# A kernel whose order comes from a planner: new job lengths, new hand-offs and new ranks

## The chip, the core and the metric

One core of a Trainium2 chip runs the whole program. Its engines are named as in the profile: PE (TensorE, matrix products), PEld (PE's weight loads), DVE (VectorE), ACT (ScalarE), POOL (GpSimd) and SP (SyncE, which only issues transfers here). The metric is the device time of one launch in microseconds (us), as the median of several runs; lower is better. A profiled execution gives the trace that is read below.

## The reference, cut to what matters

```python
x = attention(q, k, v)              # (2, 12, 448, 64), causal, softmax over keys
x = x.transpose(0, 2, 1, 3).reshape(896, 768)
h = x @ w_in                        # 768 -> 2048
P = a[0] + a[1]*h + a[2]*h*h + a[3]*h**3
Q = 1.0 + abs(b[0])*abs(h) + abs(b[1])*h*h
x = (P / (Q + 1e-6)) @ w_out        # 2048 -> 768
gate = 1.0 / (1.0 + exp(-(x @ w_gate)))
out = (gate * (x @ w_val)) @ w_out2 # 768 -> 1536 -> 768
```

Attention comes first, then a feed-forward layer with a rational function (weights `in`, `out`), then a gated one (weights `gate`, `val`, `out2`).

## The kernel before

**Attention** works on twelve pairs of heads, numbered 0 to 11: six for the first batch of tokens, six for the second. The 448 tokens are cut into four row tiles of 112, gathered in three groups: row tiles 0 and 1, row tile 2, row tile 3. A pair goes through these steps. PE makes the scores of a group (`s`, line 442). DVE adds the mask and takes the maximum of each row (`e`, `sc`, line 450). ACT takes the exponential (line 464). PE transposes the result (`p`, line 482). DVE copies the first and third group out of PSUM (line 492), ACT the second (line 490). PE multiplies by v, one product for each of four key tiles (`x`, line 519, of 448, 336, 224 and 112 columns). On the side DVE inverts the row sums (lines 470 and 471), PE spreads them (`r`, line 501), ACT copies them out (line 511), and DVE multiplies `x` by them (`xn`, line 528). ACT and POOL split the result into a high and a low part (`xh`, line 535; `xl`, line 540). There is one PSUM buffer for `x`: the first `x` product of the next pair has to wait until DVE's line 528 has read the last one. `s` and `p` share two PSUM buffers.

**Feed-forward products** come as triples high x high, high x low, low x high: `h` in lines 256 to 258, `o` in lines 314 to 316, `z` in lines 379 to 381. The first `h` and `o` tiles need only the first batch of tokens, so their triples are put between attention's matmuls and keep PE busy there. A weight is split on the way in: SP loads it, ACT takes two passes (lines 157 and 161), DVE joins the words (`val`, line 164), ACT or POOL rounds (lines 172 and 174) and POOL subtracts (line 176). ACT and DVE also evaluate the rational function on each `h` tile (lines 271 to 287).

**The order** on every engine is made while the program is built. Each step is a `Job` with an engine, a length in microseconds (`cost`), jobs that it waits for, and a rank. `in_turn` plays the jobs through: the engine that can start first takes, among its ready jobs, the one of lowest rank; a job's result is available to another engine a `handoff` later. The order that comes out is fixed in the program (each instruction is tied behind the one before it on its engine). On the chip an engine keeps that order and waits for real results, so the lengths decide the order alone and not the time. The ranks are `rank + R_...`, a pair's place in time plus an offset for each kind of step (`R_MAX`, `R_EXP`, `R_COPY`, `R_X` and so on); weight steps have `R_W`, `W_AT` and `W_STEP`.

Of the kernel before, what the change touches and what calls it, by code (L numbers as in the profile page):

```python
# [35 lines left out]
def in_turn(named, handoff):  # L36

    free = {}
    waiting = {}
    jobs = list({id(j): j for j in named.values()}.values())  # L40
    for j in jobs:
        deps = [named[d] for d in j.deps if d in named]
        j.waits = len(deps)
        for d in deps:
            d.then.append(j)
    for j in jobs:
        free.setdefault(j.engine, 0.0)
        waiting.setdefault(j.engine, [])
        if not j.waits:
            waiting[j.engine].append(j)  # L50
    for _ in jobs:
        now, e = min((max(free[e], min(j.ready for j in w)), e) for e, w in waiting.items() if w)
        job = min((j for j in waiting[e] if j.ready <= now), key=lambda j: j.rank)
        waiting[e].remove(job)
        free[e] = now + job.cost
        for j in job.then:
            j.ready = max(j.ready, free[e] + (handoff[e] if j.engine != e else 0.0))
            j.waits -= 1
            if not j.waits:
                waiting[j.engine].append(j)  # L60
        yield job
# [8 lines left out]
def tile_causal_attention__moe_rational__moe_glu(  # L70
# [16 lines left out]
    B, NP, P, _, S = qk.shape  # L87
    CP, NQ, _, D = v.shape[2:]
# [8 lines left out]
    NT = B * S  # L97
# [21 lines left out]
    for i in range(N_WARM):  # L119
# [7 lines left out]
        out=mask[:, S - CP :],  # L127
# [92 lines left out]
    CUT = S // P * P  # L220
# [189 lines left out]
    GROUPS = [(0, 1), (2,), (3,)]  # L410
# [132 lines left out]
    J = {}  # L543

    def job(key, engine, cost, deps, rank, emit, *args):
        J[key] = Job(engine, cost, deps, rank, lambda: emit(*args))
# [4 lines left out]
    def freed_by(ring, back=2):  # L551
        k = len(freed[ring]) - back
        return freed[ring][k] if k >= 0 else []
# [1 line left out]

    NG = len(GROUPS)
    LA = 2
    R_TURN, R_R, R_X, R_W = -11.0, -16.0, 34.0, -3.5
    R_MAX, R_COPY, R_INV, R_XN = -14.5, -9.5, 7.0, 12.5
    R_EXP, R_ROUT = 6.25, -42.5  # L560
    W_AT, W_STEP = 9, 5
    R_SUM = 9.5
    EXP = (0.39, 0.48, 0.57, 0.67)
    MAX = (0.28, 0.39, 0.51, 0.62)
    COPY = (0.39, 0.62, 0.70, 1.09)
    both = range(2)
    for it in range(len(pairs) * NG + LA):
        n, k = divmod(it, NG)
        rank = it * NQ / NG
        if n < len(pairs):  # L570
            if k == 0:
                job(("load", n), "SP", 3.0, [("x", n - 3, NQ - 1)], (n - 2) * NQ, load, n)
            job(
                ("s", n, k),
                "PE",
                sum(0.187 * (t + 1) + 0.05 for t in GROUPS[k]) + 0.25,
                [("load", n), *freed_by("s")],
                rank - 37.5,
                scores,
                n,  # L580
                k,
            )
            for t in GROUPS[k]:
                for j in both:
                    job(("max", n, t, j), "DVE", MAX[t] + 0.08, [("s", n, k), ("p", n - 1, k)], rank + R_MAX, maximum, n, k, t, j)
                    job(("exp", n, t, j), "ACT", EXP[t] + 0.19, [("max", n, t, j), ("r", n - 3)], rank + R_EXP, exponentials, n, t, j)
            freed["s"].append([("max", n, t, j) for t in GROUPS[k] for j in both])
        if it < LA:
            continue
        n, k = divmod(it - LA, NG)  # L590
        rank = (it - LA) * NQ / NG
        job(
            ("p", n, k),
            "PE",
            sum(0.2 * (t + 1) for t in GROUPS[k]) + 0.1,
            [("exp", n, t, j) for t in GROUPS[k] for j in both] + freed_by("s"),
            rank + R_TURN,
            turn,
            n,
            k,  # L600
        )
        for t in GROUPS[k]:
            job(("copy", n, t), "ACT" if t == 2 else "DVE", COPY[t], [("p", n, k), ("x", n - 2, NQ - 1)], rank + R_COPY, copied, n, k, t)
        freed["s"].append([("copy", n, t) for t in GROUPS[k]])
        if k < NG - 1:
            continue
        job(("inv", n), "DVE", 0.4, [("exp", n, t, j) for t in range(NQ) for j in both], rank + R_INV, inverses, n)
        job(("r", n), "PE", 0.9, [("inv", n), ("r out", n - 1)], rank + R_R, factors, n)
        job(("r out", n), "ACT", 0.52, [("r", n), ("hi", n - 1), ("lo", n - 1)], rank + R_ROUT, factors_out, n)
        for kt in range(NQ):  # L610
            deps = [("copy", n, t) for t in range(kt, NQ)] + [("x", n, kt - 1) if kt else ("xn", n - 1)]
            job(("x", n, kt), "PE", 0.187 * (NQ - kt) + 0.15, deps, rank + R_X + kt / 2, values, n, kt)
        job(("xn", n), "DVE", 0.62, [("x", n, NQ - 1), ("r out", n)], rank + R_XN, result, n)
        job(("hi", n), "ACT", 0.57, [("xn", n)], rank + 1, result_hi, n)
        final = pairs[n][1] == NP - 1
        job(("lo", n), "DVE" if final else "POOL", 0.62 if final else 1.14, [("hi", n)], rank + 1, result_lo, n)


    def coefficients():
# [18 lines left out]

    job("late", "", 0.0, [k for k in J if k != "ab"], 0, late)

    UNIT2 = 0.525
    UNIT = {S: 0.615, CUT: 0.525, NT - CUT: 0.69}

    STAGES = [("SP", 4.0), ("ACT", 0.92), ("ACT", 0.9), ("DVE", 1.3), ("ACT", 0.84), ("POOL", 2.0)]
    portions = []

    def portion(key, w, free, rank):
        p = len(portions)
        portions.append(key)
        for m, (engine, cost) in enumerate(STAGES):  # L650
            if m == 4 and key[0] in BY_POOL:
# [80 lines left out]
        follow(key, stages, rank, [*free, *deps])  # L732
        n_tmp.append((key, len(stages) - 1))

    RATIONAL = [("ACT", 1.9), ("DVE", 2.0), ("ACT", 1.28), ("DVE", 2.05), ("ACT", 0.56), ("POOL", 1.3)]
    GLU = [("ACT", 0.62), ("DVE", 0.62), ("ACT", 0.56), ("POOL", 1.25)]

    def scaled(stages, c, b, more=0.0):
        f = width(c, b) / S
# [2 lines left out]
    def stage_in(c, b):  # L742

        groups = [(0, 1), (2,), (3,)] if (c, b) == (0, 0) else [(i,) for i in range(NF)]
        for group in groups:
            keys = [("in", c, b, i) for i in group]
            deps = [place(k, 1) for k in keys]
            for u in range(KC):
                for k, d in zip(keys, deps):
                    w = [("in", c, k[3] // 2, u // 3, 5), ("lo", b * NP + u)]  # L750
                    matmuls(k, u, d + w, UNIT[width(c, b)], in1_tile)
            for k in keys:
                followed(k, scaled(RATIONAL, c, b), ("out", c, b, 0, "mm", k[3]))
            yield

    def stage_out(c, b):
        stages = [("ACT", 0.53) if c == 0 else ("DVE", 0.62)]
        if c == NCH - 1:
            stages += [("ACT", 0.56), ("POOL", 1.25)]
        for e in range(KC):  # L760
            key = ("out", c, b, e)
            deps = place(key, 0)
            for i in range(NF):
                matmuls(key, i, deps + [("out", c, i, 0, 5), ("in", c, b, i, "after", 5)], UNIT[width(c, b)], out1_tile)
            follow(key, scaled(stages, c, b, 0.15 * (c > 0) * b), at["end"] + R_SUM)
            yield

    def stage_in2(c, b):
        for i in range(NF2):
            kg, kv = ("gate", c, b, i), ("val", c, b, i)  # L770
            for key, make in ((kg, gate_tile), (kv, val_tile)):
                deps = place(kv, 0 if key == kg else 1)
                for u in range(KC):
                    w = [(key[0], c, 0, u // 3, 5), ("out", NCH - 1, b, u, "after", 2)]
                    matmuls(key, u, deps + w, UNIT[width(1, b)], make)

            followed(kv, scaled(GLU, 1, b), ("out2", c, ready[b], 0, "mm", i), [("in", NCH - 1, 1, NF - 1, "after", 2)])
            yield

    def stage_out2(c, b):  # L780
        stages = [("ACT", 0.48) if c == 0 else ("DVE", 0.55)]
        if c == NCH2 - 1:
            stages.append(("SP", 0.1))

        sums = [("out", NCH - 1, k, KC - 1, "after", 2) for k in range(B)]
        for m in range(ready[b], ready[b + 1]):
            for n in range(2):
                key = ("out2", c, m, n)
                deps = place(key, 0) + sums
                for i in range(NF2):  # L790
                    gs = [("val", c, k, i, "after", 3) for k in range(b + 1)]
                    matmuls(key, i, deps + [("out2", c, i, 0, 5), *gs], UNIT2, out2_tile)
                follow(key, stages, at["end"] + R_SUM)
                yield
# [40 lines left out]
            j.rank = at[j.rank]  # L835

    latest = {}
    for j in in_turn(J, {"PE": 0.2, "DVE": 0.1, "ACT": 0.12, "POOL": 0.12, "SP": 0.1, "": 0.0}):
        traced = nc.cur_bb.bb.instructions
        before = len(traced)  # L840
        j.emit()
        for ins in traced[before:]:
            if ins.engine in latest:
                tc.add_manual_dep(
                    ins,
                    latest[ins.engine].name,
                    mybir.DependencyInfo(mybir.DependencyClass.NoSync, mybir.DependencyReason.DATA),
                    reason="in turn",
                )
            latest[ins.engine] = ins  # L850
# [43 lines left out]
```

## Time and profile before

| | us |
|---|---|
| median of 3 runs (602.89 to 604.39) | 602.94 |
| the profiled execution | 603.39 |
| its span, first to last instruction | 601.4 |
| PE busy | 593.5 (99%) |
| DVE busy | 358.0 (60%) |
| ACT busy | 357.2 (59%) |
| POOL busy | 254.4 (42%) |

The profiled execution took 603.39 us, of which 1.99 lie around the span. Attention's work ends about 126 us into the span; the rest is feed-forward work. A matmul's end is modelled in the profile, so PE's busy time also covers waits that are shorter than what the model adds; the chain of waits, which shows how far each piece carried the run forward, gives a better price for a block of matmuls.

### The profile page before, as it was taken

The numbers are of one execution on the slowest core, as the hardware profiler recorded it, in microseconds if no ns is written. First come the engines' busy times: TensorE is split into PE (matmuls) and PEld (weight loads), VectorE is DVE, ScalarE is ACT, GpSimd is POOL, SyncE is SP. The second block draws the span as 40 slices with busy tenths as digits, with TensorE's granted clock in tenths as the row PEclk, the third lists the DMA queues.
The fourth block names the chain that finished last, engine by engine and source line by source line (L and its number), as shares of the span: only waits on it lengthen the run. The fifth ranks groups of instructions, "written<-read, shape, count | busy, mean of one in ns | idle before, by whom it ended". The sixth has DMA issues, their size and how long they took to land.

```text
span 601.4 us, 8821 instructions
## 1 busy us (share of the span) xinstructions
PE 593.5 (99%) x3352; PEld 511.6 (85%) x3352; DVE 358.0 (60%) x677; ACT 357.2 (59%) x686; POOL 254.4 (42%) x193
## 2 busy tenths in 40 slices
PE   7999999999999999999999999999999999999997
PEld 5566666689988998898898989989989989989987
DVE  5877899938968986789685243246336335312314
ACT  6888888858897793859396448766344444111010
POOL 0634321357529656534746465545145144211010
PEclk9999999999999999999999999999999999999999
DMA  7645340045413351323421054645324123000004
GB/s 242 207 173 158 118 166 16 6 157 166 146 53 110 108 195 53 113 88 123 152 59 51 2 158 158 210 157 161 102 105 159 54 105 106 0 1 1 0 14 170
DMA packets 25641, 65.05 MB, mean 108 GB/s; under 512 B 1984, under 2 KB 3776, under 8 KB 25600
## 3 DMA queue, kind: packets, MB, share of 16 engines
q1 hardware_dynamic: 25600, 64.50, 32.7%
q8 instruction: 26, 0.43, 0.3%
q14 instruction: 15, 0.12, 0.1%
HBM read 61.74 MB, written 2.75 MB: 107 GB/s over the span
## 4 chain that ended last, share of the span: by engine, by line
PE 97%; DVE 2%; issue 0%; ACT 0%; DVEq 0%
PE h L256 7%; PE o L314 6%; PE h L258 6%; PE h L257 6%; PE o L315 6%; PE o L316 6%; PE z L381 5%; PE z L379 5%; PE z L380 5%; PE gu L257 5%; PE gu L258 5%; PE gu L256 5%; PE vu L257 5%; PE vu L256 5%; PE vu L258 5%; PE s L442 4%
## 5 line engine op out<-in xcount | busy, mean ns | idle before, releaser
L361 POOL TENSOR_TENSOR gl<-pr_u,gh 128x384 fp32r<-128x384 f32 (+1 forms) x24 | 27.7, 1153 | 111.5 <-ACT gh L359 111.5
L289 POOL TENSOR_TENSOR gl_h<-t_h,gh_h 128x384 fp32r<-128x384 f32 (+2 forms) x32 | 39.2, 1226 | 84.0 <-ACT gh_h L287 83.9
L256 PE MATMUL h<-xh,wh_in 128*128 128x384 f32 (+2 forms) x192 | 71.3, 371 | 0.0
L314 PE MATMUL o<-gh_h,oh_out 128*128 128x384 f32 (+2 forms) x192 | 70.3, 366 | 0.0
L315 PE MATMUL o<-gl_h,oh_out 128*128 128x384 f32 (+2 forms) x192 | 69.9, 364 | 0.0
L316 PE MATMUL o<-gh_h,ol_out 128*128 128x384 f32 (+2 forms) x192 | 69.9, 364 | 0.0
L258 PE MATMUL h<-xh,wl_in 128*128 128x384 f32 (+2 forms) x192 | 69.7, 363 | 0.0
L257 PE MATMUL h<-xl,wh_in 128*128 128x384 f32 (+2 forms) x192 | 69.7, 363 | 0.0
L176 POOL TENSOR_TENSOR ol_out<-val_out,oh_out 128x768 fp32r<-128x768 f32 x28 | 55.1, 1971 | 26.7 <-ACT oh_out L174 25.4
L389 DVE TENSOR_TENSOR y<-y,z 128x384 f32<-128x384 f32 x70 | 38.3, 552 | 32.2 <-PE z L381 32.1
L357 DVE TENSOR_TENSOR pr_u<-sg_u,vu 128x384 f32<-128x384 f32 (+1 forms) x24 | 14.8, 617 | 70.8 <-PE vu L258 68.4
L381 PE MATMUL z<-oh_out,gl 128*128 128x384 f32 x168 | 56.2, 335 | 0.0
L379 PE MATMUL z<-oh_out,gh 128*128 128x384 f32 x168 | 56.2, 335 | 0.0
L380 PE MATMUL z<-ol_out,gh 128*128 128x384 f32 x168 | 56.2, 334 | 0.0
L164 DVE SCALAR_TENSOR_TENSOR val_out<-raw_out 128x768 uint32<-128x768 uint32 x28 | 35.7, 1277 | 31.3 <-ACT raw_out L161 23.4
L464 ACT ACTIVATE e<-e,sc 112x112 f32<-112x112 f32 (+3 forms) x96 | 49.7, 522 | 6.5 <-DVE sc L450 6.3
L258 PE MATMUL gu<-xh,wl_gate 128*128 128x384 f32 (+1 forms) x144 | 52.2, 363 | 0.0
L257 PE MATMUL gu<-xl,wh_gate 128*128 128x384 f32 (+1 forms) x144 | 52.2, 363 | 0.0
L257 PE MATMUL vu<-xl,wh_val 128*128 128x384 f32 (+1 forms) x144 | 52.1, 362 | 0.0
L256 PE MATMUL gu<-xh,wh_gate 128*128 128x384 f32 (+1 forms) x144 | 52.1, 362 | 0.0
L256 PE MATMUL vu<-xh,wh_val 128*128 128x384 f32 (+1 forms) x144 | 52.1, 362 | 0.0
L258 PE MATMUL vu<-xh,wl_val 128*128 128x384 f32 (+1 forms) x144 | 52.1, 362 | 0.0
(89 smaller groups left out, 1425.5 us busy)
## 6 DMA issues: line engine op xcount, KB each, us to landing
raw_out<-in_moe_w_out_dram SPq DMA_DIRECT2D x28, 768.0 KB, 4.3
raw_in<-in_moe_w_in_dram SPq DMA_DIRECT2D x16, 768.0 KB, 4.5
raw_gate<-in_moe_w_gate_dram SPq DMA_DIRECT2D x12, 768.0 KB, 4.3
raw_val<-in_moe_w_val_dram SPq DMA_DIRECT2D x12, 768.0 KB, 4.3
qk<-in_qk_dram SPq DMA_DIRECT2D x12, 448.0 KB, 5.7
v<-in_v_dram SPq DMA_DIRECT2D x12, 224.0 KB, 3.8
out_dram<-y SPq DMA_DIRECT2D x14, 192.0 KB, 1.8
a_sb<-in_moe_a_dram SPq DMA_DIRECT2D x1, 2.0 KB, 7.1
```

What stands on the lines that cost most here:

```text
L176: nc.gpsimd.tensor_tensor(lo, vf, hi, op=ALU.subtract)
L256: nc.tensor.matmul(ps, hi[:, c, fs], xh[:, c, bs], start=(c == 0), stop=False)
L257: nc.tensor.matmul(ps, hi[:, c, fs], xl[:, c, bs], start=False, stop=False)
L258: nc.tensor.matmul(ps, lo[:, c, fs], xh[:, c, bs], start=False, stop=(c == KC - 1))
L289: nc.gpsimd.tensor_tensor(gl, t, gh, op=ALU.subtract)
L314: nc.tensor.matmul(ps, hi[:, es], gh, start=(i == 0), stop=False)
L315: nc.tensor.matmul(ps, hi[:, es], gl, start=False, stop=False)
L316: nc.tensor.matmul(ps, lo[:, es], gh, start=False, stop=(i == NF - 1))
L379: nc.tensor.matmul(ps, gh[:, ms], hi[:, ns], start=(i == 0), stop=False)
L380: nc.tensor.matmul(ps, gh[:, ms], lo[:, ns], start=False, stop=False)
L381: nc.tensor.matmul(ps, gl[:, ms], hi[:, ns], start=False, stop=(i == NF2 - 1))
L464: nc.scalar.activation(e, e, AF.Exp, bias=d["sc"][:, t, j : j + 1], scale=-1.0, accum_out=d["sum"][:, t, j : j + 1])
```

## The change

No instruction is added, removed or altered. The numbers in the planner are replaced: the lengths of jobs (an exponential loses the 0.19 that was added to it, a maximum its 0.08; DVE's joining of weight words goes from 1.3 to 0.95; ACT's weight passes from 0.92 and 0.9 to 0.83 and 0.81; the two long DVE jobs of the rational function from 2.0 and 2.05 to 1.82 and 1.85), the hand-offs (DVE 0.1 to 0.18, ACT 0.12 to 0.2, POOL 0.12 to 0.15, PE 0.2 to 0.15) and all rank offsets. Of the diff a few lines stand for the rest:

```diff
-    R_TURN, R_R, R_X, R_W = -11.0, -16.0, 34.0, -3.5
-    R_MAX, R_COPY, R_INV, R_XN = -14.5, -9.5, 7.0, 12.5
+    R_TURN, R_R, R_X, R_W = -11.5, -27.0, 32.5, -12.0
+    R_MAX, R_COPY, R_INV, R_XN = -25.5, -20.5, 26.0, 3.5
...
-                    job(("exp", n, t, j), "ACT", EXP[t] + 0.19, [("max", n, t, j), ("r", n - 3)], rank + R_EXP, exponentials, n, t, j)
+                    job(("exp", n, t, j), "ACT", EXP[t], [("max", n, t, j), ("r", n - 3)], rank + R_EXP, exponentials, n, t, j)
...
-    STAGES = [("SP", 4.0), ("ACT", 0.92), ("ACT", 0.9), ("DVE", 1.3), ("ACT", 0.84), ("POOL", 2.0)]
+    STAGES = [("SP", 4.0), ("ACT", 0.83), ("ACT", 0.81), ("DVE", 0.95), ("ACT", 0.75), ("POOL", 1.9)]
...
-    for j in in_turn(J, {"PE": 0.2, "DVE": 0.1, "ACT": 0.12, "POOL": 0.12, "SP": 0.1, "": 0.0}):
+    for j in in_turn(J, {"PE": 0.15, "DVE": 0.18, "ACT": 0.2, "POOL": 0.15, "SP": 0.1, "": 0.0}):
```

All five engines get a new order; three places of it follow. In the names the first number of `s_2_1`, `p_2_0`, `x_1`, `xn_...` and `e_2_3_0` counts pairs, the second of `s` and `p` is the group, the second of `e` the row tile; the last number only counts buffers.

The first place is PE from the third pair's last scores to the second pair's first `x` products. Before:

```order
L442 MATMUL s_2_2_374<-qk_0_2_181 112x448 x2
L482 MATMUL p_2_0_378<-ident_102,e_2_0_0_313 112x112
L482 MATMUL p_2_0_378<-ident_102,e_2_0_1_322 112x112
L482 MATMUL p_2_0_378<-ident_102,e_2_1_0_325 112x112 x2
L482 MATMUL p_2_0_378<-ident_102,e_2_1_1_337 112x112 x2
L519 MATMUL x_1_390<-pt_0_1_156,v_0_1_152 64x448 x2
L519 MATMUL x_1_390<-pt_0_1_156,v_0_1_152 64x336 x2
```

Now, on the same engine:

```order
L442 MATMUL s_2_2_360<-qk_0_2_184 112x448 x2
L482 MATMUL p_2_0_364<-ident_102,e_2_0_0_309 112x112
L482 MATMUL p_2_0_364<-ident_102,e_2_0_1_311 112x112
L482 MATMUL p_2_0_364<-ident_102,e_2_1_0_323 112x112 x2
L482 MATMUL p_2_0_364<-ident_102,e_2_1_1_325 112x112 x2
L519 MATMUL x_0_286<-pt_0_0_149,v_0_0_145 64x224 x2
L519 MATMUL x_0_286<-pt_0_0_149,v_0_0_145 64x112 x2
L482 MATMUL p_2_1_398<-ident_102,e_2_2_0_344 112x112 x3
L482 MATMUL p_2_1_398<-ident_102,e_2_2_1_350 112x112 x3
L519 MATMUL x_1_407<-pt_0_1_156,v_0_1_152 64x448 x2
```

The last two `x` products of pair 0, which stood far ahead of this place, have moved to just before the first of pair 1, with one transposition between them.

The second place is DVE at the same time, around line 528 of pair 0. Before:

```order
L164 SCALAR_TENSOR_TENSOR val_in0_0_3_372<-raw_in0_0_3_274 128x768
L528 TENSOR_TENSOR xn_0_266<-xn_0_266,x_0_288 128x448
L450 ISA e_2_3_0_388,sc_0_2_186<-s_2_2_374,mask_107 112x448
L450 ISA sc_0_2_186 112x1
L450 ISA e_2_3_1_395,sc_0_2_186<-s_2_2_374,mask_107 112x448
L450 ISA sc_0_2_186 112x1
L492 COPY pt_0_2_187<-p_2_0_378 112x2x112
L492 COPY pt_0_2_187<-p_2_0_378 112x2x2x112
```

Now, on DVE:

```order
L450 ISA e_2_3_0_371,sc_0_2_189<-s_2_2_360,mask_107 112x448
L450 ISA sc_0_2_189 112x1
L450 ISA e_2_3_1_376,sc_0_2_189<-s_2_2_360,mask_107 112x448
L450 ISA sc_0_2_189 112x1
L164 SCALAR_TENSOR_TENSOR val_in0_0_3_381<-raw_in0_0_3_297 128x768
L492 COPY pt_0_2_190<-p_2_0_364 112x2x112
L492 COPY pt_0_2_190<-p_2_0_364 112x2x2x112
L528 TENSOR_TENSOR xn_0_267<-xn_0_267,x_0_286 128x448
```

Line 528 of pair 0 stood ahead of the third pair's last maxima; it has moved behind them, behind the joining of weight words and behind two copies.

The third place is PE near the end of attention, around the last pair's second transposition. Before:

```order
L442 MATMUL s_11_2_1436<-qk_1_5_1230 112x448 x2
L519 MATMUL x_10_1443<-pt_1_4_1109,v_1_4_1105 64x448 x2
L519 MATMUL x_10_1443<-pt_1_4_1109,v_1_4_1105 64x336 x2
L519 MATMUL x_10_1443<-pt_1_4_1109,v_1_4_1105 64x224 x2
L519 MATMUL x_10_1443<-pt_1_4_1109,v_1_4_1105 64x112 x2
L482 MATMUL p_11_1_1464<-ident_102,e_11_2_0_1412 112x112 x3
```

Now, on the same engine:

```order
L519 MATMUL x_10_1433<-pt_1_4_1140,v_1_4_1136 64x448 x2
L442 MATMUL s_11_2_1443<-qk_1_5_1169 112x448 x2
L501 MATMUL r_10_1446<-ident_102,sum_1_4_1138 64x112 x8
L482 MATMUL p_11_0_1458<-ident_102,e_11_0_0_1393 112x112
L482 MATMUL p_11_0_1458<-ident_102,e_11_0_1_1397 112x112
L482 MATMUL p_11_0_1458<-ident_102,e_11_1_0_1399 112x112 x2
L482 MATMUL p_11_0_1458<-ident_102,e_11_1_1_1410 112x112 x2
L519 MATMUL x_10_1433<-pt_1_4_1140,v_1_4_1136 64x336 x2
L482 MATMUL p_11_1_1475<-ident_102,e_11_2_0_1424 112x112 x3
```

The four `x` products of pair 10, which stood together between the last scores and this transposition, are now cut into three pieces around it, and `r` of pair 10 and the first transposition of pair 11 have come between.

## Rows read from the trace of the kernel before

**Rows 1.** The page's first part: busy us, share of the span, instructions.

```profile
PE 593.5 (99%) x3352; PEld 511.6 (85%) x3352; DVE 358.0 (60%) x677; ACT 357.2 (59%) x686; POOL 254.4 (42%) x193
```

**Rows 2.** Busy us by stretch: PE, PEld, DVE, ACT, POOL; granted clock, DMA share, GB/s.

```profile
0.00:14.00 14.00, 10.94 (x82) 8.04 (x84) 6.89 (x36) 8.92 (x29) 1.38 (x9) 1.00 0.76 253
14.00:104.00 90.00, 89.75 (x699) 55.61 (x699) 75.45 (x226) 75.91 (x210) 33.66 (x26) 1.00 0.42 141
104.00:126.00 22.00, 20.94 (x160) 14.21 (x161) 17.24 (x42) 17.99 (x42) 4.92 (x4) 1.00 0.21 67
126.00:300.00 174.00, 174.00 (x869) 157.81 (x868) 137.13 (x209) 125.84 (x212) 103.52 (x74) 1.00 0.36 117
```

**Rows 3.** The waits of PE: us in total, times, longest.

```profile
PE s L442 <- DVE sc L450: 1.8, 3, 0.8
...
PE p L482 <- DVE sc L450: 0.7, 1, 0.7
```

**Rows 4.** The chain of waits, 102 to 120 us: start, us, what (x counts matmuls).

```profile
107.66 0.73 ACT pt L490
...
113.66 1.44 DVE t_h L285
115.10 0.53 DVE e L450
...
116.33 0.76 PE p L482 x6
```

**Rows 5.** The whole chain of waits, three pieces of `x`.

```profile
41.95 1.47 PE x L519 x8
...
44.90 0.72 PE x L519 x8
...
81.20 2.04 PE x L519 x16
```

**Rows 6.** The chain of waits, 45 to 51 us: first matmuls of two triples.

```profile
45.62 0.41 PE h L256
...
49.63 0.21 PE h L256
```

**Rows 7.** The chain of waits, 84 to 89 us.

```profile
86.75 0.77 PE p L482 x8
```

**Rows 8.** The chain of waits, 14 to 24.5 us.

```profile
17.48 0.72 PE p L482 x6
...
19.29 0.91 PE p L482 x8
...
20.54 0.75 PE s L442 x4
21.30 0.92 PE r L501 x16
22.21 0.94 PE s L442 x4
```

**Rows 9.** The timeline, 4.5 to 24 us: start, us, engine, line, operation.

```profile
14.88 0.61 DVE L450 CUSTOM_DVE_ANT_0 e<-s,mask 112x448 f32<-112x448 f32 x1
...
15.97 0.92 DVE L492 COPY pt<-p 112x224 f32<-112x224 f32 x2
...
17.36 0.20 ACT L464 ACTIVATION_READ_ACCUMULATOR e<-e,sc 112x1 f32 x1
...
23.07 0.61 DVE L528 TENSOR_TENSOR xn<-xn,x 128x448 f32<-128x448 f32 x1
```

**Rows 10.** Three lines of DVE, 0 to 126 us: duration ns min/median/max, first and last start.

```profile
L164 DVE SCALAR_TENSOR_TENSOR val_in<-raw_in x6: 906/953/1272, 16.8 to 121.5; 128x768 uint32<-128x768 uint32 x6
...
L285 DVE SCALAR_TENSOR_TENSOR t_h<-d_h,t_h x4: 624/624/1441, 80.8 to 113.7; 128x448 f32<-128x448 f32 x4
...
L470 DVE TENSOR_SCALAR sum<-sum x12: 159/168/1773, 11.1 to 117.5; 112x8 f32<-112x8 f32 x12
```

**Rows 11.** The timeline, 104 to 126 us.

```profile
113.15 1.48 POOL L540 TENSOR_TENSOR xl<-xn,xh 128x448 fp32r<-128x448 f32 x1 [4.54 <-ACT xh L535]
```

More of the change, by code (lines that the diff above doesn't have):

```diff
@@ L557, in tile_causal_attention__moe_rational__moe_glu @@
     LA = 2
-    R_TURN, R_R, R_X, R_W = -11.0, -16.0, 34.0, -3.5
-    R_MAX, R_COPY, R_INV, R_XN = -14.5, -9.5, 7.0, 12.5
[L560 to L565, printed above, removed]
+    R_TURN, R_R, R_X, R_W = -11.5, -27.0, 32.5, -12.0
+    R_MAX, R_COPY, R_INV, R_XN = -25.5, -20.5, 26.0, 3.5
+    R_EXP, R_ROUT = -3.25, -56.0
+    W_AT, W_STEP = 10, 6
+    R_SUM = 13.5
+    EXP = (0.39, 0.47, 0.57, 0.66)
+    MAX = (0.2, 0.31, 0.43, 0.55)
+    COPY = (0.31, 0.54, 0.62, 1.01)
     both = range(2)
@@ L575, in tile_causal_attention__moe_rational__moe_glu @@
                 "PE",
-                sum(0.187 * (t + 1) + 0.05 for t in GROUPS[k]) + 0.25,
+                sum(0.187 * (t + 1) for t in GROUPS[k]) + 0.2,
                 [("load", n), *freed_by("s")],
-                rank - 37.5,
+                rank - 51.0,
                 scores,
@@ L584, in tile_causal_attention__moe_rational__moe_glu @@
                 for j in both:
-                    job(("max", n, t, j), "DVE", MAX[t] + 0.08, [("s", n, k), ("p", n - 1, k)], rank + R_MAX, maximum, n, k, t, j)
-                    job(("exp", n, t, j), "ACT", EXP[t] + 0.19, [("max", n, t, j), ("r", n - 3)], rank + R_EXP, exponentials, n, t, j)
+                    job(("max", n, t, j), "DVE", MAX[t], [("s", n, k), ("p", n - 1, k)], rank + R_MAX, maximum, n, k, t, j)
+                    job(("exp", n, t, j), "ACT", EXP[t], [("max", n, t, j), ("r", n - 3)], rank + R_EXP, exponentials, n, t, j)
             freed["s"].append([("max", n, t, j) for t in GROUPS[k] for j in both])
@@ L594, in tile_causal_attention__moe_rational__moe_glu @@
             "PE",
-            sum(0.2 * (t + 1) for t in GROUPS[k]) + 0.1,
+            sum(0.19 * (t + 1) for t in GROUPS[k]) + 0.06,
             [("exp", n, t, j) for t in GROUPS[k] for j in both] + freed_by("s"),
@@ L608, in tile_causal_attention__moe_rational__moe_glu @@
         job(("r", n), "PE", 0.9, [("inv", n), ("r out", n - 1)], rank + R_R, factors, n)
-        job(("r out", n), "ACT", 0.52, [("r", n), ("hi", n - 1), ("lo", n - 1)], rank + R_ROUT, factors_out, n)
+        job(("r out", n), "ACT", 0.43, [("r", n), ("hi", n - 1), ("lo", n - 1)], rank + R_ROUT, factors_out, n)
         for kt in range(NQ):
             deps = [("copy", n, t) for t in range(kt, NQ)] + [("x", n, kt - 1) if kt else ("xn", n - 1)]
-            job(("x", n, kt), "PE", 0.187 * (NQ - kt) + 0.15, deps, rank + R_X + kt / 2, values, n, kt)
-        job(("xn", n), "DVE", 0.62, [("x", n, NQ - 1), ("r out", n)], rank + R_XN, result, n)
-        job(("hi", n), "ACT", 0.57, [("xn", n)], rank + 1, result_hi, n)
+            job(("x", n, kt), "PE", 0.187 * (NQ - kt) + 0.05, deps, rank + R_X + kt / 2, values, n, kt)
+        job(("xn", n), "DVE", 0.55, [("x", n, NQ - 1), ("r out", n)], rank + R_XN, result, n)
+        job(("hi", n), "ACT", 0.47, [("xn", n)], rank + 1, result_hi, n)
         final = pairs[n][1] == NP - 1
-        job(("lo", n), "DVE" if final else "POOL", 0.62 if final else 1.14, [("hi", n)], rank + 1, result_lo, n)
+        job(("lo", n), "DVE" if final else "POOL", 0.55 if final else 1.14, [("hi", n)], rank + 1, result_lo, n)
     def coefficients():
@@ L639, in tile_causal_attention__moe_rational__moe_glu @@
     job("late", "", 0.0, [k for k in J if k != "ab"], 0, late)
-    UNIT2 = 0.525
-    UNIT = {S: 0.615, CUT: 0.525, NT - CUT: 0.69}
-    STAGES = [("SP", 4.0), ("ACT", 0.92), ("ACT", 0.9), ("DVE", 1.3), ("ACT", 0.84), ("POOL", 2.0)]
+    UNIT2 = 0.521
+    UNIT = {S: 0.64, CUT: 0.521, NT - CUT: 0.68}
+    STAGES = [("SP", 4.0), ("ACT", 0.83), ("ACT", 0.81), ("DVE", 0.95), ("ACT", 0.75), ("POOL", 1.9)]
     portions = []
@@ L733, in followed @@
         n_tmp.append((key, len(stages) - 1))
-    RATIONAL = [("ACT", 1.9), ("DVE", 2.0), ("ACT", 1.28), ("DVE", 2.05), ("ACT", 0.56), ("POOL", 1.3)]
-    GLU = [("ACT", 0.62), ("DVE", 0.62), ("ACT", 0.56), ("POOL", 1.25)]
+    RATIONAL = [("ACT", 1.55), ("DVE", 1.82), ("ACT", 1.08), ("DVE", 1.85), ("ACT", 0.47), ("POOL", 1.16)]
+    GLU = [("ACT", 0.53), ("DVE", 0.55), ("ACT", 0.47), ("POOL", 1.16)]
     def scaled(stages, c, b, more=0.0):
@@ L756, in stage_out @@
     def stage_out(c, b):
-        stages = [("ACT", 0.53) if c == 0 else ("DVE", 0.62)]
+        stages = [("ACT", 0.44) if c == 0 else ("DVE", 0.56)]
         if c == NCH - 1:
-            stages += [("ACT", 0.56), ("POOL", 1.25)]
+            stages += [("ACT", 0.47), ("POOL", 1.16)]
         for e in range(KC):
@@ L780, in stage_out2 @@
     def stage_out2(c, b):
-        stages = [("ACT", 0.48) if c == 0 else ("DVE", 0.55)]
+        stages = [("ACT", 0.4) if c == 0 else ("DVE", 0.48)]
         if c == NCH2 - 1:
```

## The prediction

> **What bounds the kernel now.** I read the page's first part, then the stretches, the waits of PE, and the chain of waits where PE does wait. PE is busy for 593.5 us of a span of 601.4, 99%, against 60% for DVE and 59% for ACT [rows 1]. By stretch [rows 2] the reader should see where the missing 8 us lie. Behind attention PE has no gap: 174.00 us of 174 from 126 us on. In the body of attention, 14 to 104 us, it is busy for 89.75 of 90, although DVE and ACT stand at 75.45 and 75.91 us there, some 84%. The gaps are at the start (10.94 of 14) and at the end of attention (20.94 of 22). PE's granted clock is 1.00 in each of these stretches, its 2.4 GHz level, so the clock is no term of this sum. The waits of PE by name [rows 3] are scores behind maxima, 1.8 us in three places, which the whole trace has before 12 us, and one transposition behind a maximum, 0.7 us, near 115 us. In the chain of waits one sees what that was [rows 4]: DVE's line 285 took 1.44 us from 113.66, the last maximum came behind it (115.10, 0.53 us), and the transposition could start at 116.33 only. ACT's copy at 107.66 stands on the chain too.
>
> Such a kernel gets shorter in two ways only: PE waits less, or its matmuls in the new order cost it less. It gets longer by either as easily. No matmul is added or removed, so I price the new order on PE by pieces of the chain of the old one, and look for places where a result that PE needs is now late.
>
> **The change part by part.** The new lengths and hand-offs cost nothing by themselves: they decide the order alone. Up to the first transposition that stands at 17.48 us in the trace, PE has the same sequence in both orders, so the waits of the start, 3.06 us of idle time before 14 us [rows 2], stay: 0. (Only DVE has two tiny jobs of the coefficients moved there.)
>
> *Term A, changes of block on PE.* The four `x` products of a pair cost 2.04 us where they stand together, and 1.47 + 0.72 = 2.19 us where they stand as two pieces [rows 5]: each separate piece costs 0.15 us more. Counted over the whole order of PE, attention's `x` products stand in 22 pieces before and in 32 now: 10 × 0.15 = +1.5 us. A triple of `h` or `o` has a first matmul of 0.41 us behind `x` or `s` and 0.21 us behind another triple [rows 6]; entries of the dear kind go from 13 to 15: 2 × 0.2 = +0.4. A third transposition costs 0.77 us behind a triple [rows 7] and 0.91 behind `x` or `r` [rows 8]; those behind a triple go from 6 to 8: 2 × 0.15 = −0.3. A = **+1.6 us**. PE has no idle time in the body that could hide it. The least I allow is 0 (a change of block costs something only where the next weights come late, and in other company it might not), the most 1.9 (without the gain on transpositions).
>
> The Trainium skill ("TensorE: Matmul & The Clock Gate", section "Back-to-back issue gap") gives the isolated gap of a warm matmul as its columns over 2.4 GHz plus 2.5 ns, and thus nothing for what stood ahead of it; an estimate by that formula alone makes A zero, against +1.6 by the rows. The rows do not bear the formula out at a change of block, where the same matmul of a triple takes 0.41 instead of 0.21 us [rows 6].
>
> *Term B, a new wait at pair 1's first `x` product.* There is one PSUM buffer for `x`, and this product waits for DVE's line 528 of pair 0. On PE the order now runs from 17.48 us: transposition 0.72, `r` of pair 1 0.92, scores of pair 2 0.75, transposition 0.91, `x` of pair 0 in a piece of one product (1344 columns altogether, like the piece of 0.72), last scores of pair 2 0.94 [rows 5, 8]. These end at 17.48 + 0.72 + 0.92 + 0.75 + 0.91 + 0.72 + 0.94 = 22.44. Then transposition 0.72, the last two `x` products of pair 0 0.72, transposition 0.72: at 24.60 PE comes to `x` of pair 1. DVE meanwhile starts the two last maxima when their scores are there, at about 22.5. In the trace two such took from 14.88 to 15.97, 1.1 us [rows 9], so they end at 23.6; line 164 takes 0.9 [rows 10], to 24.5; two copies 0.85 (0.92 as busy time [rows 9]), to 25.35; line 528 some 0.55 to 0.6 [rows 9], to 25.9; a hand-off of less than 0.1 makes it 26.0. PE waits 26.0 − 24.6 = **+1.4 us**. In the order before, line 528 stood ahead of the maxima and the wait did not arise. The least is 1.0, with every DVE job at its shortest and PE 0.2 later; the most 2.2, if line 164 is lengthened as line 285 was, 0.62 to 1.44 us [rows 10]. Behind the waiting `x` product on PE stand the third transposition of pair 2 and the scores of pair 3, so all of attention moves by this amount. On ACT the splitting of `xn` (line 535) stands ahead of the copy of pair 2's second group, which is late by as much, but is wanted only by scores some 2 us later.
>
> *Term C, the waits at the end of attention.* PE's idle time between 104 and 126 us is 22 − 20.94 = 1.06 us [rows 2]; a few hundredths are hidden under the modelled ends at each of three waits, so I put 1.3 on it. All three belong to an order in which transpositions, scores and inverses of pairs 10 and 11 wait for DVE and ACT in turn [rows 4]. In the new one the first transposition of pair 11, `r` of pair 10 and one `x` product lie between the last scores and the second transposition, DVE's line 285 is not directly ahead of the last maxima, and by the prices above what PE needs is ready 0.5 to 1.2 us early. C = **−1.3 us**; the least gain is 0, if waits of the same kind come back elsewhere.
>
> *Term D, small waits in the body.* Priced by the same pieces, the time from the end of a group's scores to its transposition was about 5.3 to 7.6 us for most pairs before and is 3.3 to 5.2 now, 2.6 at one place (second group of pair 3). The path itself, maxima and exponentials of 448 columns with empty queues, took from 14.88 to 17.56, 2.7 us [rows 9]; for the 336 columns of the second group I estimate 2.3. So margins of several microseconds have become margins of about one, and one DVE job of 0.9 us in between uses one up. And DVE jobs get longer now and then: line 285 to 1.44 from 0.62, line 470 to 1.77 from 0.17 [rows 10], the former while POOL ran line 540 for 1.48 us [rows 11]. I count the lengthened jobs of this kind as three in attention before, of which one reached PE, for 0.8 us. With thinner margins I expect one such hit, or two of half its size, less the chance that none comes: D = **+0.5 us**; bounds 0 and 2.4 (three hits of 0.8).
>
> The Trainium skill ("SBUF — State Buffer", section "Who interferes with whom") says that DVE and GpSimd share a pair of ports under an exclusive lock. The trace agrees in that line 285 was lengthened just while line 540 ran on POOL [rows 10, 11]. By a full lock line 285 would have lost the 0.97 us for which line 540 still ran (113.15 + 1.48 − 113.66); it lost 0.82. An estimate by the rule alone puts the upper bound of D at 2.9 instead of 2.4.
>
> *Behind 126 us* I put 0: PE has no wait there, DVE is at 137.13 of 174 [rows 2], and the triples have the same shapes.
>
> **Sum.** 1.6 + 1.4 − 1.3 + 0.5 = +2.2 us. The profiled execution took 603.39 us, 601.4 of them span; the changed one should have a span of 603.6 and take 605.6 us. The median of the runs is 0.45 lower than the profiled execution, so the forecast is 602.94 + 2.2 = **605.1 us**.
>
> **The rivals.**
>
> *Changes of block cost nothing* (A = 0): for it speaks that in other company the next weights may be there in time, and that the skill's formula has no such price; against it that the two ways of `x` in the trace differ by 0.15 us [rows 5]. Then +0.6: 603.5 us. Chance 0.08.
>
> *The other side: the late waits go and the new ones do not come.* B decides: if line 528 of pair 0 ends by 24.6 us, or PE is slower to that place than I price it, B and D are 0, and 1.6 − 1.3 = +0.3 remains: 603.2 us; with B half there 603.9. Against it stands that DVE keeps its order, with 1.1 + 0.9 + 0.85 us of work between the scores and line 528. Chance 0.22.
>
> *Attention gains more than that.* If A were 0 as well and C went fully, the time would be 602.94 − 1.3 = 601.6, still within 0.3%; under that bound it comes only if the waits of the start shrink too, or the triples behind 126 us become cheaper. Nothing in the order shows either. Chance 0.07, put at 600.8.
>
> *The waits move behind attention.* The offset of the sums out of PSUM behind 126 us goes from 9.5 to 13.5 and weight steps come earlier (−3.5 to −12). DVE has 37 us to spare in 174 there; if copies out of PSUM come late behind weight work, PE waits for a buffer. The trace shows no such wait now, so its size has no row; with four to seven waits of 0.8, as the one near 115 us [rows 3], it is +3 to +6 us: 606 to 611. Chance 0.10.
>
> My forecast has the remaining 0.53.
>
> **How the numbers follow.** 0.3% is 1.8 us, about what a measurement of this kernel can tell from no change: slower begins at 604.75, faster at 601.13. The likeliest case has its own range of 603.9 to 606.8 (A between 1.0 and 1.9, B between 1.0 and 2.2, C between −1.3 and −0.6, D between 0 and 1.5); some three tenths of it lie under 604.75. Same: 0.08 + 0.22 + 0.02 of the faster rival + 0.16 of the forecast, less 0.05 in which the second rival has B nearly whole = 0.43. Slower: 0.37 + 0.10 + 0.05 = 0.52. Faster: 0.05. The range goes from 602.6, which leaves out the gaining rival, to 607.5, which leaves out the larger half of the waits behind attention.
>
> **What would show it.** In the changed profile `x` should appear in more and shorter pieces on the chain, of 0.72 and 0.90 us instead of 2.04 (A). `x` of pair 1 should wait for DVE's line 528 near 24.6 us for about 1.4 us, and everything behind it should stand later by as much (B). Between 104 and 126 us PE should have almost no idle time (C). DVE instructions of more than 1.4 us directly ahead of a wait of PE would be D. Behind attention PE should be busy throughout. I am wrong on the whole if PE's busy time in attention does not grow, if no wait is seen near 25 us, or if PE waits behind 126 us.

## The result, and the profile after

The changed kernel takes 607.31 us (median of four runs, 606.53 to 607.49), the kernel before 603.36 in the same comparison (602.89 to 604.39). The ratio is 1.0061, with a 95% interval of 1.0043 to 1.0078: slower by 3.7 us, give or take one. The forecast was 605.1 us, slower, with a range of 602.6 to 607.5.

The busy time by stretch (window, length, PE, PEld, DVE, ACT, POOL; granted clock, DMA share, GB/s) of the changed kernel:

```profile
14.00:104.00 90.00, 87.95 (x678) 54.15 (x678) 76.59 (x226) 80.75 (x212) 33.28 (x26) 1.00 0.47 158
104.00:126.00 22.00, 22.00 (x177) 14.01 (x178) 16.81 (x47) 15.32 (x40) 4.58 (x4) 1.00 0.01 1
126.00:300.00 174.00, 173.25 (x868) 157.44 (x867) 131.27 (x207) 122.78 (x209) 97.99 (x73) 1.00 0.34 111
300.00:345.00 45.00, 44.26 (x221) 39.48 (x220) 26.25 (x43) 27.87 (x48) 24.21 (x23) 1.00 0.21 66
```

Against [rows 2] the idle time of PE has moved. The body of attention has 90 − 87.95 = 2.05 us where it had 0.25. The end of attention has none where it had 1.06. Behind attention there are 0.75 and 0.74 us where there were none. ACT is 4.8 us busier in the body of attention (80.75 against 75.91): its weight passes, lines 157 and 161, run 24 times there against 17. The waits of PE by name:

```profile
PE s L442 <- DVE sc L450: 1.9, 4, 0.6
PE o L315 <- POOL gl_h L289: 1.5, 2, 0.7
PE x L519 <- issue: 1.4, 1, 1.4
```

The third row is the wait that the prediction placed near 25 us. The chain of waits, 14 to 34 us, has it behind the transposition that ends at 25.53; the profile calls it "issue" there, and names no releaser:

```profile
18.41 0.72 PE p L482 x6
...
22.42 0.94 PE s L442 x4
...
24.80 0.73 PE p L482 x6
25.53 1.39 issue
26.92 1.54 PE x L519 x8
...
30.66 0.77 PE r L501 x16
31.42 0.19 PE x L519 x4
```

The timeline of DVE, 22 to 28 us, names what PE waited for: the maxima, line 164, the copies and line 528 in the order that the change gave them. Line 528 ends at 26.82, and `x` starts at 26.92.

```profile
23.96 0.62 DVE L450 CUSTOM_DVE_ANT_0 e<-s,mask 112x448 f32<-112x448 f32 x1
...
24.50 0.95 DVE L164 SCALAR_TENSOR_TENSOR val_in<-raw_in 128x768 uint32<-128x768 uint32 x1
25.38 0.92 DVE L492 COPY pt<-p 112x224 f32<-112x224 f32 x2
26.21 0.61 DVE L528 TENSOR_TENSOR xn<-xn,x 128x448 f32<-128x448 f32 x1
```

**An account of the 4.1 us between the two profiled spans** (605.5 − 601.4). The first term is the start, where the order of PE is the same in both kernels. The transposition of [rows 8] at 17.48 us stands at 18.41: +0.93. The chain of the first 19 us shows why, first of the changed kernel, then of a kernel of the experiments (`dense_old`) whose attention is ordered in the same way:

```profile
1.18 3.78 PE warm L120 x16
4.96 1.42 PE s L442 x8
```

```profile
1.18 3.52 PE warm L120 x16
4.71 0.79 PE s L442 x8
```

The first scores took 1.42 us in one execution and 0.79 in the other. Those 0.9 us belong to an execution and not to the order: of this case's profiles with the new start some have them and some don't, and so it is with the old start (`b_x_cut`, below, has the same 1.42). The Trainium skill ("TensorE: Matmul & The Clock Gate", section "Part 1: The HAM clock gate") calls the number of slow matmuls at a kernel's start variable from run to run; the two pairs of rows agree in that the first matmuls take longer in one execution than in the other. That the clock is the reason is not shown: the granted clock reads 1.00 in both.

The second term is attention. The first `h` triple of the second batch stands behind the same set of matmuls in both orders: all those of attention, with the `h` and `o` triples that are put between them. By the timeline, 134 to 142 us, it starts here in the kernel before, and below that in the changed one:

```profile
134.06 0.37 PE L256 MATMUL h<-xh,wh_in 128*128 128x448 f32 x1
```

```profile
136.48 0.36 PE L256 MATMUL h<-xh,wh_in 128*128 128x448 f32 x1
```

That is +2.42, and without the start +1.49 us. The rest, 4.1 − 2.42 = 1.7 us, comes behind attention, of which the idle time above is 1.49. The split is good to some 0.3 us: measured at other triples the distance falls from 2.54 us at 128 to 2.17 at 150, because the profiled execution of the kernel before takes a little longer for each matmul there. `b_x_cut`, which has that kernel's order behind attention, does not, so this too belongs to an execution.

### The profile page after: what moved, and what is told of

Same layout as the page of the kernel before. It is cut to its first block, busy times and chain, and to the rows that moved or that the text cites. A ratio compares the mean times of both kernels' runs of the same rounds, so it can differ in the third digit from the quotient of the medians.

```text
span 605.5 us, 8838 instructions
## 1 busy us (share of the span) xinstructions
PE 595.5 (98%) x3352; PEld 512.3 (85%) x3352; DVE 353.3 (58%) x677; ACT 355.8 (59%) x686; POOL 252.4 (42%) x193
## 4 chain that ended last, share of the span: by engine, by line
PE 82%; DVE 7%; ACT 4%; DMA 3%; POOL 2%; issue 1%; DVEq 0%; POOLq 0%; ACTq 0%; SPq 0%
PE z L381 5%; PE z L379 5%; PE z L380 5%; PE gu L258 5%; PE gu L257 5%; PE gu L256 5%; PE vu L256 5%; PE vu L258 5%; PE vu L257 5%; PE o L315 5%; PE o L314 5%; PE o L316 5%; PE s L442 4%; PE x L519 4%; PE p L482 4%; PE h L256 4%
## 5 line engine op out<-in xcount | busy, mean ns | idle before, releaser
L289 POOL TENSOR_TENSOR gl_h<-t_h,gh_h 128x384 fp32r<-128x384 f32 (+2 forms) x32 | 37.0, 1155 | 78.2 <-ACT gh_h L287 78.2
L164 DVE SCALAR_TENSOR_TENSOR val_out<-raw_out 128x768 uint32<-128x768 uint32 x28 | 34.0, 1215 | 25.5 <-ACT raw_out L161 18.2
```

## The experiments

In each of them the order of all jobs that the planner makes is kept as one list, `sequence`, edited, and then issued. `turns(True)` is the list made with the new numbers, `turns(False)` with the old ones; `moved(seq, keys, ahead)` puts jobs ahead of another. The times of before on the same chips were 603.5 to 603.8 us.

| kernel | us | ratio to before, 95% interval |
|---|---|---|
| `xn0_ahead` | 607.78 | 1.0066 (1.0051 to 1.0081) |
| `xn0_first` | 606.58 | 1.0053 (1.0038 to 1.0068) |
| `x_together` | 610.70 | 1.0121 (1.0104 to 1.0138) |
| `b_x_cut` | 606.20 | 1.0041 (1.0027 to 1.0054) |
| `b_x_together` | 608.52 | 1.0083 (1.0070 to 1.0097) |
| `dense_old` | 605.52 | 1.0028 (1.0018 to 1.0038) |
| `attention_old` | 610.25 | 1.0100 (1.0078 to 1.0121) |
| `gh_ahead` | 606.41 | 1.0053 (1.0036 to 1.0070) |
| `rest_old_lengths` | 606.26 | 1.0042 (1.0028 to 1.0055) |
| `lengths_new` | 617.57 | 1.0233 (1.0218 to 1.0249) |
| `ranks_new` | 605.04 | 1.0029 (1.0017 to 1.0041) |
| `tail_new` | 615.48 | 1.0196 (1.0182 to 1.0210) |

**The wait near 25 us.** First by moving what it waits for:

```diff
 sequence = turns(True)
+sequence = moved(sequence, [("x", 0, 2), ("x", 0, 3), ("xn", 0)], ("s", 2, 2))
```

> The order of now, with one edit: the last two x products of pair 0 go ahead of the third pair's last scores on PE, and line 528 of pair 0 ahead of that pair's last maxima on DVE, as before the change. If the wait near 25 us is a cost of its own: PE has no wait there, everything behind it stands 1.4 us earlier, and 0.15 more for one piece of x less, so about 605.8 us instead of 607.3. If DVE's load only moves the wait along (rival): another wait of PE of about the same size appears in the next 20 us, and the time stays near 607.3.

It took 607.78 us: nothing gained. The waits of PE now have the last two of these in place of the one of 1.4, and the first, behind attention, has grown from 1.5 us:

```profile
PE o L315 <- POOL gl_h L289: 2.1, 2, 1.4
...
PE r L501 <- ACT xn L511: 0.8, 1, 0.8
PE p L482 <- DVE sc L450: 0.7, 1, 0.7
```

The rival was right. A transposition had to wait for maxima that now came later, and `r` for ACT's line 511, which waits for POOL's line 540, which stood behind weight work. Before the end of attention the gain was used up; why the wait behind attention grew as well was not followed up. The second try leaves PE alone and takes the weight work out of the way instead:

```diff
 sequence = turns(True)
+sequence = moved(sequence, [("xn", 0)], ("copy", 2, 0))
+sequence = moved(sequence, [("hi", 0)], ("in", 0, 1, 0, 1))
+sequence = moved(sequence, [("in", 0, 0, 1, m) for m in (3, 4, 5)], ("in", 0, 1, 1, 0))
+sequence = moved(sequence, [("lo", 0)], ("in", 0, 0, 1, 4))
```

> The order of now, PE's and ACT's nearly unchanged: line 528 of pair 0 goes ahead of the joining of weight words and the two copies on DVE, line 535 of pair 0 ahead of one weight pass on ACT, and that weight's lines 164, 172 and 176 behind line 540 of pair 0. If weight work in front of attention's chain makes the wait near 25 us: PE waits there at most 0.2 us and nowhere else instead, about 605.9. If the wait only moves on, as when the x products were moved (rival): one or two waits of 0.5 to 1 us in the next 6 us, near 607.3.

The wait near 25 us was gone. Two thirds of the gain came back some 8 and 16 us later (0.4 and 0.5 us), the second part as its chain, 23 to 42 us, shows:

```profile
28.66 2.42 POOL wl_in L176
...
38.94 1.24 DVE sum L470
...
40.20 0.21 DVE sum L471
...
40.46 0.99 PE r L501 x16
```

The weight steps that were put off fell together with the next ones on POOL and DVE, and `r` waited for an inverse that took 1.24 us instead of 0.17 while POOL ran line 176. The idle time between 300 and 345 us grew too, from 0.74 to 1.18 us. At 606.58 us the kernel cannot be told from the changed one. So the wait is real, and its cause is the one predicted, but neither of two better places removed its cost. DVE and ACT have little room in that stretch of the changed kernel, 18 to 42 us (busy for 20.12 and 21.38 of 24 us), POOL has more (13.32). Whether some other order there would keep the gain is open.

**The price of a piece of `x`.** Each pair's products are put together at the place of the last:

```diff
+for n in range(len(pairs)):
+    sequence = moved(sequence, [("x", n, kt) for kt in range(NQ - 1)], ("x", n, NQ - 1))
```

in the new order:

> The order of now, with each pair's four x products kept together at the place of the last one: 12 pieces instead of 32. If a piece costs 0.15 us: 20 times 0.15 = 3.0 us less of matmul time in attention, and the wait near 25 us goes too, since the first x product of pair 1 comes later; what stood between the pieces comes up to 1.5 us earlier and may wait, so between 603 and 605.3 us. If pieces cost nothing (rival): 1.4 us less at the most, 605.9 or more.

and in the old one:

> The order of before, with each pair's four x products kept together at the place of the last one: 12 pieces instead of 22. If a piece costs 0.15 us: 1.5 us less of PE's own time, and since this order has longer margins than the new one, at most half of it comes back as waits: 0.7 to 1.5 us under before, faster than both kernels. If the waits of DVE's and ACT's results take it all back (rival), as they did in the new order with x together: as before or 1 to 2 us over it.

610.70 and 608.52 us: the waits took back much more than the theories had in mind. The waits of PE for the maxima, of the first and of the second kernel, say where it went:

```profile
PE s L442 <- DVE sc L450: 5.6, 10, 1.1
```

```profile
PE s L442 <- DVE sc L450: 5.5, 9, 1.3
```

Scores wait for maxima and transpositions for copies, because the `x` products that stood between them were what PE did while DVE worked. The reverse, more pieces in the old order and nothing else, tells the price:

```diff
+pe = [k for k in sequence if J[k].engine == "PE"]
+for n in range(1, len(pairs) - 1):
+    last = ("x", n, NQ - 1)
+    i = pe.index(last)
+    if pe[i - 1][0] != "x":
+        i = pe.index(("x", n, 1))
+    if pe[i - 1][0] == "x" and pe[i + 1][0] != "x":
+        k = pe[i]
+        sequence.remove(k)
+        sequence.insert(sequence.index(pe[i + 1]) + 1, k)
```

> The order of before with one thing of the new order alone: more pieces of x. In eight pairs the matmul block behind the last x product changes places with that product, so that x stands in 30 pieces instead of 22; transpositions and scores come at most 0.4 us earlier, where they had 3 us to spare, and results of x 0.9 us later. If a piece costs 0.15 us of PE's own time: 8 times 0.15 = 1.2 us, and up to 0.4 for other changes of block, so 1.2 to 1.6 us over before, with no new wait. If the price was one of waiting and not of changing blocks (rival): as before within 0.3 us.

The edit moves nine products. Eight make a new piece; the one of pair 1 makes none, but puts pair 3's first scores one product ahead. 606.20 us, 2.4 over before, of which 0.4 is a wait of these scores near 26 us: their `qk`, issued no later than before but for the slow start (19.18 us against 18.24), landed at 25.92. The list of waits has nothing between 38 and 96 us, so the price can be read there. In `b_x_cut`, 35 to 41 us and 92 to 99 us:

```profile
39.59 0.34 PE x L519 x4
39.93 0.91 PE p L482 x8
```

```profile
97.53 0.34 PE x L519 x4
97.87 0.76 PE s L442 x8
```

and the same transposition and the same scores in the kernel before:

```profile
38.47 0.91 PE p L482 x8
```

```profile
95.10 0.76 PE s L442 x8
```

The distance grows from 39.93 − 38.47 = 1.46 to 97.87 − 95.10 = 2.77 over six cuts: 1.31 us. Six times the predicted 0.15 make 0.9. One cut also made an entry of an `h` triple a dear one: 0.2. The remaining 0.2 is a wait after all, too short for the list, here in the chain of `b_x_cut`, 76 to 83 us, and in its timeline, 78.5 to 81.2 us:

```profile
80.55 0.46 PE h L256
```

```profile
80.53 0.19 PEld L256 LDWEIGHTS h<-xh,wh_in 128*128 128x128 f32 x1 [0.20 <-DVE t_h L277]
```

This triple stands behind a transposition, where its first product takes 0.22 us in the kernel before. It begins a new `h` tile and waited for DVE's line 277, the last reader of the tile that had its PSUM buffer. Eight cuts at 0.15, the dear entry, this wait, the transfer and 0.2 more of waiting near 118 us make 2.2 of the 2.4 us. So the price of a change of block is PE's own time, and of the predicted size; what the pieces bring for it is cover.

**The rest, behind attention.** One order up to the end of attention, the other from there:

```diff
+first, second = turns(True), turns(False)
+first = first[: first.index("late") + 1]
+sequence = first + [k for k in second if k not in set(first)]
```

> The order of now on all engines up to the end of attention, and from there the order of before for all that is left. If the two waits of o for POOL's line 289 behind attention are made by the new order of the weight passes and of the rational function there: they are gone, and the time is about 1.4 us lower, 605.9. If they come from the state in which attention leaves the engines (rival): they stay, near 607.3.

605.52 us, and its busy time by stretch has no idle time of PE behind attention:

```profile
126.00:300.00 174.00, 174.00 (x872) 158.04 (x871) 135.22 (x208) 124.42 (x210) 101.75 (x73) 1.00 0.35 114
300.00:345.00 45.00, 45.00 (x224) 40.21 (x223) 24.33 (x42) 28.85 (x50) 23.89 (x26) 1.00 0.16 52
```

So the two waits are made by the order behind attention. What is left over before, 1.7 us by the times, fits attention's 1.5. The chain of the changed kernel shows the first place (140 to 170 us) and the second (312 to 324):

```profile
163.27 0.82 ACT raw_out L157
164.09 0.79 ACT raw_out L161
164.88 0.46 ACT gh_h L287
...
165.41 1.15 POOL gl_h L289
```

```profile
309.85 5.14 DMA raw_gate<-in_moe_w_gate_dram
...
315.01 0.91 ACT raw_gate L157
315.92 0.51 ACT gh_h L287
```

ACT makes two passes over weights that nobody waits for, and only then line 287, for which POOL's line 289 and then `o` wait. At the second place it even stands still for a transfer ahead of line 287. Moving these passes behind it:

```diff
+sequence = moved(sequence, [("out", 1, 1, 0, 1), ("out", 1, 1, 0, 2)], ("in", 1, 0, 1, "after", 0))
+sequence = moved(sequence, [("gate", 1, 0, 0, 1)], ("out", 3, 0, 0, "after", 1))
```

> The order of now with two edits on ACT behind attention: the two passes over weights (lines 157 and 161) that stand ahead of line 287 of the h tile that o waits for near 166 us go behind it, and so does line 157 of a weight that waits for its transfer at 313 us. If these steps ahead of line 287 make the two waits of o for line 289: both waits of PE are gone, 1.5 us by the list of waits, and the time is 1.5 to 1.8 us lower, some 605.6 instead of 607.3. If ACT or POOL has too much to do there (rival): waits of the same size come back at the next tiles or at weights that are late, near 607.3.

The first wait was gone, and the second 0.3 us long, by its list of waits:

```profile
PE o L315 <- POOL gl_h L289: 0.3, 1, 0.3
```

At 606.41 us the time fell by less than expected, and its interval overlaps that of the changed kernel: the trace shows the cause, the time alone does not. With the lengths of before behind attention, and the new hand-offs and offset of the sums:

> The order of now up to the end of attention; the rest planned with the new hand-offs and the new offset of the sums, but with the lengths of before. If the shorter lengths put weight passes ahead of line 287: no wait of o for line 289, and as with the whole old rest, about 605.5. If the hand-offs or the offset do it (rival): the two waits stay, 607.3.

606.26 us, half of each: the wait near 166 us was gone, the one near 325 us stayed, with 0.7 us by the list of waits. The first is made by the shorter lengths; what makes the second, the hand-offs or the offset, was not parted.

The other way round:

> The reverse: the order of before up to the end of attention, and from there the order of now. If attention and the rest add up: PE has attention's waits of before, and the two waits for line 289 of now, about 1.4 us over before, 604.8. If the waits behind attention need the new attention ahead of them (rival): as before, 603.4.

610.25 us, over both theories: the two orders do not add up. Its busy time by stretch, 164 to 176 us, shows why:

```profile
164.00:167.00 3.00, 0.98 (x2) 0.53 (x3) 2.97 (x5) 3.00 (x7) 1.14 (x1) 0.76 0.49 135
167.00:172.20 5.20, 5.20 (x15) 4.59 (x15) 4.92 (x10) 4.77 (x10) 1.01 (x1) 0.50 0.63 225
```

The old attention has done fewer weight passes at its end (lines 157 and 161 have run 22 times by 126 us, 24 times with the new one), and behind it ACT's passes hold line 287 up longer. PE stands still for 2.02 of 3 us, the granted clock falls to 0.50, its 1.2 GHz level, and a matmul of `o` takes 0.37 us where it takes 0.20 at full clock, for 5.2 us. The wait costs 2 us and the clock 2.6 more in this execution, of 610.77 us; the one of the four whose mean granted clock stayed at 0.999 took 607.83.

**Lengths or ranks.** Attention made with one half of the change, the rest as before (`ranks` names the numbers that are taken from the other set):

```diff
+first, second = turns(True, ranks), turns(False)    # lengths_new: ranks of before
+first, second = turns(False, ranks), turns(False)   # ranks_new: ranks of now
```

> Attention ordered with the new lengths and hand-offs but the ranks of before; from the end of attention on the order of before. x stands in 31 pieces in that order (22 before, 32 now), and the margins are as thin as now. If the lengths and hand-offs make attention slower: about as with the new attention and the old rest, 605.5, with a wait of PE near 25 us. If the ranks make it (rival): as before, 603.8.

> Attention ordered with the new ranks but the lengths and hand-offs of before; from the end of attention on the order of before. x stands in 25 pieces and the times from scores to transpositions are as long as before. If the lengths and hand-offs make attention slower: no wait of PE near 25 us, 602.5 to 604. If the ranks make it (rival): 605.5.

The new lengths with the old ranks took 617.57 us, with the same wait of 1.4 us near 25 us and much more besides; here are its two longest entries in the list of waits, and its busy time from 122 to 130 us:

```profile
PE o L314 <- DVE t_h L277: 3.3, 1, 3.3
PE o L314 <- ACT gh_h L287: 2.9, 2, 1.8
```

```profile
122.00:130.00 8.00, 3.94 (x12) 2.19 (x11) 3.92 (x7) 3.63 (x7) 3.18 (x4) 0.72 0.00 0
```

The body of attention, 14 to 104 us, has PE busy for 87.68 us, as with both halves (87.95). The long waits stand at the end of attention, from 122 us on, and at 180 us, in the old order that follows, and the granted clock falls with them.

The new ranks with the old lengths have no wait near 25 us, and took 605.04 us. They have a wait of 1.2 us near 117 us, where the last pair's `x` follows its third transposition at once. The list names ACT's line 281, which `x` does not read; it starts at 118.17, just behind DVE's copy of that group:

```profile
116.97 1.09 DVE L492 COPY pt<-p 112x896 f32<-112x896 f32 x1
```

So the wait near 25 us comes with the lengths and hand-offs, and that part of the first theory holds. Its times do not: each half alone is slower than before, the ranks by 1.5 us, about what the rival said, the lengths by 14. With both halves and the same old order behind attention (`dense_old`) it is 1.7, so on the new lengths the new ranks take some 12 us back. How much of the 14 us lies in the lengths, and how much in the seam to the old order, was not parted.

**A try at something faster.**

```diff
+first, second = turns(False), turns(True)
+sequence = first[: first.index(("x", 8, 3)) + 1]      # order of before
+sequence += [k for k in second[: second.index("late") + 1] if k not in set(sequence)]
+sequence += [k for k in first if k not in set(sequence)]
```

> The order of before, but for the last three pairs of attention, which follow the order of now; the rest as before. x stands in 24 pieces. By the prices so far the three late waits of before go (1.36 us) and PE's own time rises by 0.8: 0.5 us under before, within what can be told from no change; if other waits come at the seam (rival), 0.5 to 1.5 over before.

615.48 us, far over both theories. The time is lost at the seam; a likely reason, not tested, is that the new order has its maxima, exponentials and weights at other distances from PE's work than the old one. Its busy time, 97 to 120 us:

```profile
101.00:109.00 8.00, 0.61 (x4) 0.62 (x4) 0.62 (x4) 5.18 (x11) 1.13 (x1) 0.50 0.42 147
109.00:115.00 6.00, 6.00 (x33) 3.87 (x31) 3.60 (x9) 4.13 (x13) 1.14 (x1) 0.54 0.00 0
```

PE waits for ACT's exponentials for 7.9 us and then has a mean granted clock of 0.54 for 6. No version of the twelve beats the kernel before.

## Why the prediction was right in sign and short in size

- **Term A, changes of block, +1.6.** The mechanism and the price of a piece held (`b_x_cut`), the size was too high by half. Attention grew by 1.49 us; its idle time by 2.05 − 0.25 − 1.06 = 0.74; so PE's own time by 0.75, or some 0.3 more, since short waits hide under the modelled ends. The reason is in the chain above: three pieces of `x` stand directly behind `r`, and such a piece costs 0.19 us for a last product instead of 0.34. They pay no price, which makes 3 × 0.15 = 0.45 less. The `r` in that chain, itself directly behind a piece of `x`, takes 0.77 us instead of the 0.92 of [rows 8], another 0.15 less. That leaves 1.0.
- **Term B, +1.4.** It came at the place and in the size: 1.39 us, behind the sequence of PE and of DVE that the prediction wrote down, each piece within 0.1 us of its price. What the prediction did not see is that undoing it freed a third of it in one try and nothing in the other.
- **Term C, −1.3.** PE has no idle time left between 104 and 126 us, 1.06 by the same count. Right.
- **Term D, +0.5.** The idle time of the body beside term B is 2.05 − 0.25 − 1.39 = 0.41. Part of it is of the sort described. Scores at 102.38 us waited for maxima behind a lengthened instruction of line 284 (it took 0.70 us at 92.54), here in the chain, 92 to 99 us, of the changed kernel:

```profile
96.20 1.53 DVE d_h L284
```

- **Behind 126 us, 0.** This step failed. It cost about 1.6 us, as two waits of `o` for POOL's line 289. The prediction looked at busy shares (DVE 137.13 of 174) and at copies out of PSUM. It did not read ACT's order there, where weight passes had moved ahead of line 287; ACT was no bound by its share either, 125.84 of 174 before. A wait of PE behind 126 us was also one of the prediction's own signs of being wrong on the whole, and it came. The rival that had waits behind attention, with a chance of 0.10, named the place, but the wrong reason (sums out of PSUM) and four to seven waits of 0.8 us where there were two; the measured 3.7 us falls into its 3 to 6 only because attention's 1.5 came on top.
- **The start** belongs to no step. One profiled execution had it and the other had not; the prediction took its zero for both.

By the profiles the sum is then 1.0 + 1.4 − 1.3 + 0.4 = 1.5 for attention, against 2.2 predicted, and 1.6 for the rest, against 0. The remainder of the 3.7 us is within the interval of the measurement. That 607.31 us lies inside the stated range is luck in part: it is above the 603.9 to 606.8 of the likeliest case, and 0.2 us under the upper end, which was set for waits behind attention of another kind.

## What to carry to other kernels

Lengths in a planner that are a little too long can be a reserve: here, with shorter lengths, it packed jobs with less slack, and what then came later (line 528 behind weight work, a transfer) ended as a wait of the bounding engine. When only an order changes, read every engine's queue over the whole program for work that nobody waits for that has moved ahead of a result that is waited for; a low busy share does not exclude it. And look beyond the place of a wait before counting on its removal: in two tries all or two thirds of the gain was lost again within some 16 us.

## What the runs showed of the hardware

- A wait of PE costs more than its length where the granted clock falls with it: after 2.02 us without work in 3, 5.2 us at 0.50 (`attention_old`); after 7.4 idle of 8 us, 6 us at 0.54 (`tail_new`). The waits of the changed kernel, one of 1.39 us and two of 0.7, left it at 1.00.
- A block of `x` directly behind `r` starts without the extra time that it has behind a triple or scores (0.19 against 0.34 us for the last product), and `r` directly behind `x` likewise (0.77 against 0.92).
- The start of one and the same order differs by up to 0.9 us between executions. That is a quarter of what was to be explained here, so marks inside two profiles are to be compared as well as their ends.
